# Attention and MLP on one core: block sums moved next to the value matmuls, one x transposed by DMA instead of TensorE, scores of even units one step on

## The chip, the cores and the metric

The kernel runs on 1 core of one Trainium2 chip. The metric is device microseconds of one execution. Before the change the median of 4 runs is 221.29 us (219.48 to 222.63). One execution was profiled; it took 220.52 us, and the profile's span of it, from the first to the last instruction, is 218.8 us.

## What is computed

```python
# q, k, v: (4, 8, 768, 64); block 32, window 16, 24 blocks
k_sum = k.reshape(B, H, nb, block, D).max(axis=3)
v_sum = v.reshape(B, H, nb, block, D).mean(axis=3)
scores_l = scale * q @ k.T          # kept where |i - j| < 16
scores_s = scale * q @ k_sum.T + log(block)
a = softmax(concat(scores_l masked, scores_s))
attn = a @ concat(v, v_sum)
x = attn.transpose(0, 2, 1, 3).reshape(3072, 512)
h = x @ w_in                        # (512, 2048)
out = (h * sigmoid(1.702 * h)) @ w_out
```

## The kernel before

The 3072 rows are cut into 8 units u of 384 rows, half a batch each: b = u // 2, half = u % 2. Each unit has an input stage and an output stage. In the input stage (`ff_in`, line 676) TensorE multiplies `w_in` by the unit's transposed x: 16 groups nt of 4 matmuls with 384 columns, and ScalarE applies the gelu into `gT`. In the output stage (`ff_out`, line 704) TensorE multiplies `gT` by `w_out` into `po`, 48 matmuls with 512 columns in 12 steps of 4; a step is (ms, part), ms being one of three blocks of 128 rows. After part 3 ScalarE copies `po` into `osb` and SP stores it.

The attention of unit u+1 is done inside the output stage of unit u. Function `beside` (line 896) is called after each step i with a plan of tokens for unit u+1: `plan0` for unit 1, `plan1` for unit 2, `odd` for odd units, `plan` for the other even ones. A token is a letter and a number:

- `s0`..`s3`, `S0`, `S1`: the scores of a pair of heads (`scores`, line 624): 24 small matmuls into `ps_s`, an exp on ScalarE into `a_sb`, a mask on VectorE. `s` in an even unit's plan is its own first half; `S` belongs to the odd unit after it.
- `v0`, `v1`: the values of two pairs (`values`, line 634): 24 small matmuls a pair into `ps_av`, then a reciprocal and a multiply on VectorE into `x2`.
- `x0`, `x1`: the x of two pairs is transposed on TensorE and copied by VectorE into `xTT` (`tx`, line 663).
- `d0`, `d1`: the same by a DMA transpose, issued from SP (`dx`, line 671).
- `t0`..`t3`: transposes of q for unit 2 (`tq1`, line 610).

`xTT[0]` holds pairs 0 and 1 and `xTT[1]` pairs 2 and 3. The first matmuls of every input stage read `xTT[0]` (k0 = 0 in `ff_in`).

The order of the work on each engine and on the SP queue is the order in which the program issues it: every call goes through `_Ordered` (line 17), which keeps program order. SP issues all loads, stores and DMA transposes but those of the weights, in one queue. In unit 1's output stage that queue has, in this order: four loads of k for batch 2 (line 1010), the store of ms 0, four loads of v for batch 2 (line 1013), the stores of ms 1 and ms 2. Behind them come the DMA transposes of k, whose input GpSimd casts in unit 2's input stage (`turn_keys`, line 924); GpSimd then casts v there too.

The block sums of v (`vsum`, line 305) are 24 matmuls with a selecting matrix `E` into `ps_vs`; `block_sums` (line 347) copies them into `vs` with four VectorE instructions; `halo_dmas` and `sum_dmas` spread the rows into the next batch's `vw`. In units 2 and 4 all of this stands after step 9 of the output stage (i == 10, line 1018).

`busy(6)` (line 341) is six matmuls of zeros, 128 columns each, ahead of the first output matmul of unit 0.

PSUM is held in pool `psb` (2 buffers, scores, block sums) and pool `pmm` (4 buffers, everything else).

Of the kernel before, what the change touches and what calls it, by code (L numbers as in the profile page):

```python
# [34 lines left out]
def kernel(  # L35
# [10 lines left out]
    B, H, S, D = q.shape  # L46
# [8 lines left out]
    NJ = S // 128  # L55
# [10 lines left out]
    pool = _Ordered(tc, nc.gpsimd)  # L66
# [16 lines left out]
    def chunks(x, b, p):  # L83

        return x[b, 2 * p:2 * p + 2].rearrange("h s d -> (h s) d").rearrange("(a p) d -> p a d", p=128)
# [12 lines left out]
    def load_q(b, p, half=None):  # L98
        if half is None:
            t = stage.tile([128, 2, NJ, D], F32, name=f"qf{p}", tag=f"qf{p}0")  # L100
            sp.dma_start(out=t.rearrange("p h j d -> p (h j) d"), in_=chunks(q, b, p))
            raw["q", p] = t
            return
        if half and p == 0:
            late[0] = stage.tile([128, NP, 2, JH, D], F32, name="qfl", tag="qfl")
            if b == 0:
                pool.dma_start(out=late[0].rearrange("p i h r d -> p (i h) (r d)"),
                               in_=q[0, :, HALF:S].rearrange("h (p r) d -> p h (r d)", r=JH))
        t = (late[0][:, p] if half else
             stage.tile([128, 2, JH, D], F32, name=f"qf{p}0", tag=f"qf{p}0"))  # L110
        raw["q", p, half] = t
        if b == 0 and half:
            return
        sp.dma_start(out=t.rearrange("p h r d -> p h (r d)"),
                     in_=q[b, 2 * p:2 * p + 2, half * HALF:(half + 1) * HALF]
                     .rearrange("h (p r) d -> p h (r d)", r=JH))
# [135 lines left out]
    def copy(eng, out, in_):  # L252
        if eng is act:
            act.activation(out=out, in_=in_, func=ACT.Copy)
        elif eng == "dve_alone":

            dve.tensor_reduce(out=out, in_=in_.unsqueeze(len(in_.shape)), axis=AX.X, op=ALU.max)
        else:
            eng.tensor_copy(out=out, in_=in_)
# [20 lines left out]
    def cast_q(eng, p, half=None):  # L280
        if half is None:
            if p % 2 == 0:
                qb2[p // 2] = castp2.tile([128, 2, NJ, 2, D], BF16, name="qb", tag="qb")
            t = qb2[p // 2][:, p % 2]
        else:
            t = castp.tile([128, JH, 2, D], BF16, name="qb", tag="qb")
        copy(eng, t.rearrange("p r h d -> p h r d"),
             raw[("q", p) if half is None else ("q", p, half)])
        cast["q", p] = t

    def rows_of(s, p, hh=None):

        hs = slice(2 * p, 2 * p + 2) if hh is None else slice(2 * p + hh, 2 * p + hh + 1)
        return vw[s].rearrange("p (j e) h c -> p j e h c", e=2)[:, :, :, hs, 0:D]

    def raw_v(p, hh=None):
        t = raw["v", p] if hh is None else raw["v", p][:, hh:hh + 1]
        return t.rearrange("p h j d -> p j h d")
# [6 lines left out]
    def vsum(s, js):  # L305

        if js[0] == 0:
            vs_ps[0] = psb.tile([128, 1024], F32, name="ps_vs", tag="big")[:, 0:2 * D]
        w5 = vw[s].rearrange("p (j e) h c -> p j e h c", e=2)
        for j in js:  # L310
            o = 20 - 4 * j
            for g in range(4):
                pe.matmul(out=vs_ps[0][32 * g:32 * g + 32, :], lhsT=E[:, o:o + 32],
                          rhs=w5[:, j, 0, 2 * g:2 * g + 2, 0:D],
                          start=(j == 0), stop=(j == NJ - 1), skip_group_check=True)
# [25 lines left out]
    def busy(n):  # L341
        ps = pmm.tile([128, 512], F32, name="ps_w", tag="mm")
        for i in range(n):
            pe.matmul(out=ps[:, 0:128], lhsT=warm[:, 0:128], rhs=warm[:, 0:128],
                      start=True, stop=True)

    def block_sums():
        for g in range(4):
            dve.tensor_copy(out=vs[0:32, 2 * g:2 * g + 2, 0:D],
                            in_=vs_ps[0][32 * g:32 * g + 32, :]  # L350
                            .rearrange("p (h d) -> p h d", d=D))
# [11 lines left out]
    def halo_odd(w5, j0, eng=sp):  # L363
        eng.dma_start(out=w5[32:48, j0:NJ, 1], in_=w5[48:64, j0:NJ, 0])
        eng.dma_start(out=w5[48:64, j0:NJ - 1, 1], in_=w5[0:16, j0 + 1:NJ, 0])
# [131 lines left out]
    def b_exp(g):  # L497
        ab = st["ab", g] = attp.tile([128, HALF], BF16, name="ab", tag="ab")
        act.activation(out=ab, in_=st["B", g][:, 0:HALF], func=ACT.Exp, scale=scale)

    def v_own(p, hh, eng):

        copy(eng, rows_of(0, p, hh)[:, :, 1], raw_v(p, hh))
# [118 lines left out]
    a_sb, x_sb, x2 = {}, {}, {}  # L622
# [107 lines left out]
    gate2 = consts.tile([128, 1], BF16, name="gate2")  # L730
# [149 lines left out]
    for p in range(NP):  # L880
# [2 lines left out]

    plan = {0: ["s0", "s1"], 3: ["v0", "s2", "s3"], 4: ["d0"], 5: ["v1", "S0", "S1", "d1"]}
    odd = {0: ["v0", "s2", "s3"], 1: ["d0"], 3: ["v1", "d1"]}

    plan1 = {0: ["t0"], 1: ["t1"], 2: ["s0", "s1"], 4: ["t2"], 5: ["t3"],
             6: ["v0", "s2", "s3"], 8: ["x0"], 9: ["v1", "S0", "S1"], 11: ["x1"]}  # L890

    plan0 = {-1: ["q0", "q1", "q2", "q3", "s0", "s1"], 3: ["v0", "s2"], 5: ["x0", "s3"], 7: ["v1"], 9: ["x1"]}

# [50 lines left out]
    for u in range(2 * B):  # L944
        b, half = u // 2, u % 2
        todo = {}
        if u == 0:
            for p in range(NP):
                todo.setdefault(12 + p // 2, []).append(lambda p=p: cast_q(dve, p, 1))
        elif u == 1:  # L950
            s = 1
            todo = {2: [lambda: tk(0, s)], 4: [lambda: tk(1, s)],
                    6: [lambda: tk(2, s)], 8: [lambda: tk(3, s)],
                    14: [lambda: halo_odd(w51, 0), lambda: vsum(s, range(NJ))],
                    15: [lambda: block_sums(), lambda: halo_even(w51, 0),
                         lambda: sum_dmas(w51, 0)]}
            for p in range(NP):
                cast_k(pool, p)
            for p in range(NP):
                cast_v(pool, s, p, 0)  # L960
                cast_v(pool, s, p, 1)
            for p in range(NP):
                cast_q1(p)
        elif half == 0 and b + 1 < B:
            todo = {0: [lambda: turn_keys(u, b + 1)]}
        elif b + 1 < B:
            s = (b + 1) % 2
            todo = {0: [lambda: turn_queries(u, s)],
                    1: [lambda: rest_k(0, s)], 3: [lambda: rest_k(1, s)],
                    6: [lambda: rest_k(2, s)], 8: [lambda: rest_k(3, s)]}  # L970
        if u == 1:
            for p in range(NP):
                clear_kx(pool, p, 0)
            clear_vw(pool, 0)
        if u:
            ff_in(u, range(3))
        for nt in range(0 if u else N0, NT):
            if u == 0 or nt > 2:
                ff_in(u, (nt,))
            for f in todo.get(nt, ()):  # L980
                f()
        nxt = u + 1 < 2 * B
        if nxt:
            exp_soon()
        if u == 0:
            beside(1, -1)
            busy(6)
        i = 0
        order = [(ms, part) for ms in range(JH) for part in range(4)]
        if u == 0:  # L990

            order = [(ms, part) for part in range(4) for ms in range(JH)]
        for ms, part in order:
            if nxt or ms < JH - 1:
                ff_out(u, ms, part)
            elif part == 0:
                ff_last(u, ms)
            if nxt:
                beside(u + 1, i)
            i += 1  # L1000
            if u == 0 and i == 1:

                sp.dma_start(out=hold, in_=w_out_sb[0:16, NT - 5, 0:16])
                for p in range(NP):
                    load_k(1, p)
                load_v(1)
                for p in range(NP):
                    load_q(1, p, 0)
                    load_q(1, p, 1)
            elif half and b + 2 < B and i == 1:  # L1010
                for p in range(NP):
                    load_k(b + 2, p)
            elif half and b + 2 < B and i == 7:
                load_v(b + 2)
            elif half == 0 and 0 < b < B - 1 and i == 7:
                for p in range(2, NP):
                    load_q(b + 1, p)
            elif half == 0 and 0 < b < B - 1 and i == 10:
                s = (b + 1) % 2
                vsum(s, range(NJ))  # L1020
                block_sums()
                w5 = vw[s].rearrange("p (j e) h c -> p j e h c", e=2)
                halo_dmas(w5, 0)
                sum_dmas(w5, 0)
# [30 lines left out]
```

The softmax here doesn't subtract the row's maximum and nothing guards it: scores larger than these inputs give would overflow.

## Time and profile before

| what | value |
|---|---|
| median of 4 runs | 221.29 us |
| the profiled execution | 220.52 us |
| its span | 218.8 us |
| PE busy | 205.2 us (94%) |
| ScalarE / VectorE / GpSimd busy | 135.2 / 92.1 / 68.3 us |
| `po` matmuls (377 recorded) | 85.6 us |
| `ph` matmuls (512) | 86.1 us |
| DMA moved | 37.15 MB, mean 170 GB/s |

PE is TensorE's matmuls, PEld its weight loads, DVE VectorE, ACT ScalarE, POOL GpSimd. In a timeline row the columns are start, duration (both us), engine, line, operation, output<-input, shapes and a count; an idle time of the engine before the row and what ended it stand in brackets. SPq is the SP queue; its durations are those of the issuing instruction, and a DMA lands later. Nearly every call has line 27, that of the helper that records the order, so groups are told apart by the names of their tiles. `ps_w` is the work of `busy`, `ps_x` that of `tx`, `ps_vs` that of `vsum`, `ps_s` scores, `ps_av` values. In tile names buffer numbers are left out, so `xT` is either half of x.

### The profile page before, as it was taken

What the parts mean: (1) busy time and instruction counts of PE and PEld (TensorE: products, weight loads), DVE (VectorE), ACT (ScalarE), POOL (GpSimd) and SP (SyncE); (2) the same over time, 40 slices, a digit from 0 to 9 for tenths busy, and PEclk for the clock granted to TensorE, in tenths of its full rate; (3) what the DMA queues carried; (4) which work ended last, traced back from release to release, by engine and by line L of the source; (5) the groups of instructions that cost most, each with busy time, mean ns of one, the idle gap of its engine ahead of it and who ended that gap; (6) DMA issues with size and microseconds to landing.
All of it is one profiled execution on the core that took longest, in us unless ns stands there. A gap on an engine that the chain in (4) does not pass through costs nothing.

```text
span 218.8 us, 4915 instructions
## 1 busy us (share of the span) xinstructions
PE 205.2 (94%) x1927; PEld 116.8 (53%) x1950; DVE 92.1 (42%) x262; ACT 135.2 (62%) x242; POOL 68.3 (31%) x169
## 2 busy tenths in 40 slices
PE   7684999999999999999999999999999999999994
PEld 3353756455655556545555455545655565456542
DVE  5797656553964750335707300619328003300000
ACT  2795778346678487842886677915787578437420
POOL 5683898014794019500600069104100000000000
PEclk9999799999999999999999999999999999999999
DMA  6999799999998999899799999999904300520012
GB/s 171 309 214 196 107 267 204 214 201 221 222 316 229 228 252 240 143 210 236 157 214 220 204 224 196 204 203 208 195 3 101 118 0 3 120 89 10 0 48 96
DMA packets 92710, 37.15 MB, mean 170 GB/s; under 512 B 77856, under 2 KB 89568, under 8 KB 92688
## 3 DMA queue, kind: packets, MB, share of 16 engines
q1 hardware_dynamic: 88272, 31.87, 70.6%
q0 software_dynamic: 4416, 4.98, 13.0%
q8 instruction: 15, 0.25, 0.5%
q14 instruction: 7, 0.06, 0.1%
HBM read 27.26 MB, written 6.29 MB: 153 GB/s over the span
## 4 chain that ended last, share of the span: by engine, by line
PE 86%; DMA 5%; SPq 4%; issue 1%; DVE 1%; POOL 0%; DVEq 0%
PE ph L27 38%; PE po L27 37%; PE ps_av L27 4%; SPq L27 4%; DMA vf<-in_v_dram 3%; PE ps_s L27 3%; DMA kf<-in_k_dram 2%; DVE qT L27 1%; PE ps_x L27 1%; PE ps_q L27 1%; PE ps_vs L27 1%; PE ps_t L27 1%; PE ps_vt L27 0%; POOL vw L27 0%; PE ps_w L27 0%
## 5 line engine op out<-in xcount | busy, mean ns | idle before, releaser
L27 PE MATMUL po<-w_out_sb,gT 128*128 128x512 bf16 (+2 forms) x377 | 85.6, 370 | 2.4 <-issue 1.7
L27 PE MATMUL ph<-xT,w_in_sb 128*128 128x384 bf16 x512 | 86.1, 327 | 0.0
L27 ACT ACTIVATE gT<-ph 128x384 bf16<-128x384 f32 x128 | 61.0, 490 | 22.3 <-PE ph L27 22.2
L27 PEld LDWEIGHTS <-w_in_sb 128*128 128x128 bf16 x512 | 49.8, 98 | 33.1 <-issue 0.4
L27 PEld LDWEIGHTS <-gT 128*128 128x128 bf16 x400 | 36.7, 98 | 38.6
L27 ACT ACTIVATE osb<-po 128x512 f32<-128x512 f32 (+1 forms) x24 | 14.1, 588 | 35.0 <-PE po L27 33.7
L27 ACT ACTIVATE a_sb<-ps_s 128x768 bf16<-128x768 f32 x32 | 24.3, 804 | 11.8 <-PE ps_s L27 11.5
L27 DVE RECIPROCAL rc<-ps_av 128x6 f32<-128x6 f32 x32 | 6.1, 190 | 51.8 <-PE ps_av L27 51.8
L27 POOL CAST vw<-vf 128x768 bf16<-128x768 f32 (+4 forms) x35 | 24.5, 758 | 6.5 <-DMA vf<-in_v_dram 4.9
L27 DVE TENSOR_TENSOR a_sb<-a_sb,mk 128x768 bf16<-128x768 bf16 x32 | 17.9, 559 | 17.5 <-ACT a_sb L27 15.9
L27 ACT ACT_TABLE_LOAD x16 | 20.5, 1283 | 1.1 <-PEq L1039 0.8
L27 POOL COPY gate<-gT 128x1 bf16<-128x1 bf16 x4 | 0.8, 190 | 60.3 <-ACT gT L27 60.3
L27 DVE TENSOR_TENSOR x<-ps_av,rc 128x384 bf16<-128x384 f32 x28 | 15.6, 558 | 1.0
L27 POOL CAST kb<-kf 128x768 bf16<-128x768 f32 (+1 forms) x15 | 11.1, 766 | 15.6 <-DMA kf<-in_k_dram 15.6
L27 DVE COPY osb<-po 128x128 f32<-128x128 f32 x1 | 0.3, 291 | 26.6 <-PE po L27 26.6
L27 PEld LDWEIGHTS <-a_sb 128*64 128x64 bf16 x384 | 8.1, 112 | 6.3 <-issue 3.0
L27 DVE TENSOR_REDUCE ks<-kx 128x24 bf16<-128x768 bf16 x12 | 11.3, 938 | 0.1
L27 DVE COPY kx<-kx 128x80 bf16<-128x80 bf16 (+4 forms) x50 | 11.0, 291 | 0.0
L27 PE MATMUL ps_av<-vw,a_sb 128*64 128x65 bf16 x384 | 10.1, 199 | 0.0
L27 PE MATMUL ps_s<-qT,kx 64*128 64x64 bf16 x384 | 9.3, 191 | 0.8 <-DVE qT L27 0.4
L27 POOL CAST qb<-qf 128x768 bf16<-128x768 f32 (+1 forms) x14 | 9.4, 696 | 0.6 <-POOL qb L27 0.3
L27 PEld LDWEIGHTS <-kx 64*128 64x128 bf16 x384 | 7.0, 95 | 3.5 <-issue 2.7
(71 smaller groups left out, 120.7 us busy)
## 6 DMA issues: line engine op xcount, KB each, us to landing
out_dram<-osb SPq DMA_DIRECT2D x23, 256.0 KB, 3.3
kf<-in_k_dram SPq DMA_DIRECT2D x12, 384.0 KB, 5.5
vf<-in_v_dram SPq DMA_DIRECT2D x12, 384.0 KB, 6.3
qf<-in_q_dram SPq DMA_DIRECT2D x8, 384.0 KB, 4.9
w_in_sb<-in_moe_w_in_dram POOLq DMA_DIRECT2D x4, 512.0 KB, 7.5
w_out_sb<-in_moe_w_out_dram POOLq DMA_DIRECT2D x4, 512.0 KB, 15.4
kf<-in_k_dram SPq DMA_DIRECT2D x8, 192.0 KB, 4.4
qf<-in_q_dram SPq DMA_DIRECT2D x8, 192.0 KB, 3.6
```

The lines of the kernel that those rows point to most:

```text
L27: r = f(*a, **kw)
```

## The change

Five edits and one function that nothing calls:

1. `plan`: `s0`, `s1` stand after step 1 instead of step 0 (units 4 and 6, so in the output stages of units 3 and 5).
2. `plan1`: the first x of unit 2 is transposed by DMA (`d0` after step 7) instead of on TensorE (`x0` after step 8).
3. `busy(6)` is gone.
4. The loads of v for batch 2, in unit 1's output stage, are issued after step 7 instead of after step 6, so behind the store of ms 1 and behind `d0`. (For batch 3 they stay.)
5. In the output stages of units 2 and 4, `vsum` stands after step 3 (right behind `v1`) and `block_sums` after step 4, instead of both after step 9. The DMAs that spread the rows stay after step 9.

```diff
+    def pool_waits(p):
+        pool.tensor_copy(out=gate2, in_=a_sb[p][:, 0, 0, 0:1])
...
-    plan = {0: ["s0", "s1"], 3: ["v0", "s2", "s3"], 4: ["d0"], 5: ["v1", "S0", "S1", "d1"]}
+    plan = {1: ["s0", "s1"], 3: ["v0", "s2", "s3"], 4: ["d0"], 5: ["v1", "S0", "S1", "d1"]}
     odd = {0: ["v0", "s2", "s3"], 1: ["d0"], 3: ["v1", "d1"]}
     plan1 = {0: ["t0"], 1: ["t1"], 2: ["s0", "s1"], 4: ["t2"], 5: ["t3"],
-             6: ["v0", "s2", "s3"], 8: ["x0"], 9: ["v1", "S0", "S1"], 11: ["x1"]}
+             6: ["v0", "s2", "s3"], 7: ["d0"], 9: ["v1", "S0", "S1"], 11: ["x1"]}
...
         if u == 0:
             beside(1, -1)
-            busy(6)
...
-            elif half and b + 2 < B and i == 7:
+            elif half and b + 2 < B and i == (8 if u == 1 else 7):
                 load_v(b + 2)
             elif half == 0 and 0 < b < B - 1 and i == 7:
                 for p in range(2, NP):
                     load_q(b + 1, p)
+            elif half == 0 and 0 < b < B - 1 and i == 4:
+                vsum((b + 1) % 2, range(NJ))
+            elif half == 0 and 0 < b < B - 1 and i == 5:
+                block_sums()
             elif half == 0 and 0 < b < B - 1 and i == 10:
                 s = (b + 1) % 2
-                vsum(s, range(NJ))
-                block_sums()
                 w5 = vw[s].rearrange("p (j e) h c -> p j e h c", e=2)
                 halo_dmas(w5, 0)
                 sum_dmas(w5, 0)
```

In the changed program PE has 24 instructions fewer (12 matmuls and their weight loads), VectorE one fewer (the copy of `ps_x` into `xT`), SP one more (the DMA transpose). ScalarE and GpSimd have the same instructions in the same order.

## The prediction

> **What bounds the kernel now.** I read the page's busy table and slices first, then the chain that ended last, then the timelines of PE and of the SP queue around the edits.
>
> ```profile
> PE 205.2 (94%) x1927; PEld 116.8 (53%) x1950; DVE 92.1 (42%) x262; ACT 135.2 (62%) x242; POOL 68.3 (31%) x169
> ...
> PE   7684999999999999999999999999999999999994
> ...
> PEclk9999799999999999999999999999999999999999
> DMA  6999799999998999899799999999904300520012
> ```
>
> From about 25 us PE is full at full clock, and the DMA engines are full too until about 150 us. So removed PE work is worth its own length, but a PE instruction that comes to depend on a DMA meets a crowded queue. The chain at the end of unit 1's output stage shows it is PE alone:
>
> ```profile
> 76.13 0.50 PE ps_av L27 x24
> 76.63 0.46 PE ps_s L27 x24
> 77.09 0.16 issue
> 77.25 1.67 PE po L27 x7
> 78.92 0.34 PE ps_x L27 x6
> 79.25 10.56 PE ph L27 x64
> ```
>
> Unit 2's input stage (`ph`) starts the moment unit 1's output stage ends. Its first matmuls read the x that the change hands to a DMA. The SP queue there:
>
> ```profile
> 69.29 4.58 SPq L27 DMA_DIRECT2D kf<-in_k_dram  x3
> 73.97 1.68 SPq L27 DMA_DIRECT2D out_dram<-osb  x1
> 75.70 6.88 SPq L27 DMA_DIRECT2D vf<-in_v_dram  x4
> 83.09 1.65 SPq L27 DMA_DIRECT2D out_dram<-osb  x2
> 84.84 6.03 SPq L27 DMA_TRANSPOSE kx<-kb  x4
> ```
>
> SP issues without a pause. The load at 70.54 took 1.56 us to issue and 6.1 us to land; stores behind loads (83.09 and 84.38) landed 4.0 and 3.3 us after issue.
>
> **The change, part by part.**
>
> *busy(6) gone.* The zeros start at 37.85 and the first `po` at 38.19 (PE timeline): 0.34 us of PE removed. Its cover: `po` reads the first quarter of w_out, which lands at 37.2 (issued 25.26, 11.9 to landing), in time. The second quarter lands at 40.5 (26.00 + 14.5); it is first read 12 matmuls of 0.216 us later, at 40.8 before and 40.4 after, so some 0.1 us may go back. No other idle time opens there, so the clock is not touched.
>
> *x0 by DMA.* Six transposes, 78.76 to 79.09 for the like of them (`x1`), 0.33 us, leave PE, and a 0.56 us copy leaves VectorE, off the path. PE would now reach unit 2's first `ph` at 79.09 - 0.34 - 0.33 = 78.4.
>
> When is the x there? Its multiply ends on VectorE at 73.45 + 0.56 = 74.0 (0.3 earlier after). SP is not free: the four k loads and the store of ms 0 hold it until 75.65, and that clock is set by the DMAs, not by PE. Next comes the store of ms 1, which used to stand behind the v loads (its copy ends at 74.9); a second store in a row issues in 0.4 us (84.38). So `d0` starts to issue at about 76.2. Its landing:
>
> ```profile
> L27 SPq DMA_TRANSPOSE xT<-x x10: 1212/1249/3633, 92.7 to 189.2; - x10
> DMA to landing us min/median/max: 2.8/4.2/5.7
> ```
>
> Two of the ten have a recorded landing: 2.8 us with an empty queue (189.24) and 5.7 us behind two loads of q (92.69). They are the ends: 79.0 and 81.9. Between them I follow the queue: the store ahead is issued at 75.7 and lands 3.3 to 4.0 us later, 79.0 to 79.7; a transpose of this size then needs what the k transposes need in a full queue, four in 6.03 us or 1.5 each: 80.5 to 81.2. DMA share backs the far end: 1.28 in 76 to 80 us against 0.81 ahead of the 5.7 us row and 0.26 around the 2.8 us one. I take 80.9, and 0.1 for PE to resume: 81.0. PE stands from 78.4 to 81.0, 2.6 us, and the stage starts 81.0 - 79.09 = **+1.9 us** later. The 0.67 us saved is inside this, as is any loss at 40.4: PE only waits less. Ends: 0.0 (79.0 + 0.1) and +2.9.
>
> The Trainium skill, "VectorE: DVE Perf Modes", section "The three transpose paths", gives 1309 ns for a 128x128 DMA transpose against 390 ns on TensorE, and its rules prefer TensorE where a PSUM destination will do, which speaks against this edit. By its 1.3 us, as an estimate, `d0` would land at 77.5, no wait would arise and the sum would be about 220.2 us on the profiled run. The trace's own shortest is 2.8 us, so the row decides.
>
> *v loads behind d0.* They issue some 0.4 + 1.5 = 1.9 us later. The last lands at 79.81 + 6.6 = 86.4, then 88.3. GpSimd casts k from 81.5 and v from 84.56, eight in 6.25 us; the last pair's casts start at about 89.2, and GpSimd shifts with PE (its gate waits for `gT`), so to 91. Covered by 2 to 3 us; uncovered, it would delay only casts whose first PE reader is the block sums, below. The k transposes behind (84.84) move to about 86.7; VectorE first reads them at 101.7. The `d0` of unit 3 (92.69) is behind them too, but moves with PE. I price all this at nothing.
>
> *Block sums earlier.* They need all v casts: 84.56 + 6.25 = 90.8 against 94.8 at the new place; in unit 4, 137.4 against 141.3. Both 4 us of slack, shifted alike. A PSUM buffer is free (exps end at 93.25). The four copies (1.18 us) move on VectorE from 100.6 to about 96.2, where it idles 4.4 us; `vs` is read by the same DMAs at the same place. PE's price by start-to-start:
>
> ```profile
> 94.26 0.57 PE L27 MATMUL ps_av<-vw,a_sb 128*64 128x65 bf16 x24
> 94.76 1.47 PE L27 MATMUL po<-w_out_sb,gT 128*128 128x512 bf16 x6
> ```
>
> Values alone take 0.50, block sums alone 0.46 (100.04 to 100.50), scores alone 0.46; values with scores behind them take 1.19 (116.74 to 117.93), with a 0.16 us "issue" gap at the end. Joined: 1.19 - 0.96, less 0.09 for the one entry saved (0.31 from the last `po` to a small group against 0.22), so +0.14. Nearest row: 24 values and 24 others without a `po` between. Twice: **+0.3**. Without the gap the join saves up to 0.15 each: -0.3. So -0.3 to +0.3.
>
> *Even scores one step on.* Same PE work. Scores start 0.87 us later, at 114.46; the exp waited for the table load and gate until 114.74 and now starts 0.40 after the scores (as 117.24 to 117.64), at 114.86: 0.12 late. The second mask ended at 116.83, now 116.95, when values (116.74 on) reach the second pair. `v1` at 119.53 shows such a touch: 0.05 us. Twice: **+0.1**, 0 to 0.2.
>
> Sum: 220.5 + 1.9 + 0.3 + 0.1 = 222.8 on the profiled run. That run is 0.8 below the median of the four, so I predict **223.6** against 221.29, +1.0%.
>
> **The rivals.**
>
> *d0 lands in time* (the other side, not slower). For it: the 2.8 us row and x ready at 73.7. If `d0` lands by about 79 us, the start of unit 2 is at -0.6 to 0, with the rest -0.3 to +0.4: 219.6 to 220.9 on the profiled run, about 221.0 by the median. It decides at a landing of 79.0. Against: in-order queue, DMA share 1.28.
>
> *The wait also drops the clock.* This one is worse:
>
> ```profile
> 18.33:21.74 3.41, 0.59 (x15) 0.41 (x13) 2.13 (x7) 1.22 (x3) 1.10 (x3) 1.00 1.23 203
> 21.75:25.16 3.41, 3.32 (x33) 2.57 (x33) 1.41 (x4) 1.79 (x6) 2.74 (x5) 0.50 0.42 55
> ```
>
> PE was idle for 2.92 us (18.92 to 21.84, waiting for a v cast) and then had 3.41 us at clock 0.50 (the last column but two). An idle of 1.34 us at 5.5 left it at 1.00. A 2.6 us wait lies between; half a clock for 3.41 us costs 1.7: 225.3. It decides where a wait fills most of one 3.41 us window; 2.6 us falls wholly in one in a quarter of the phases.
>
> The Trainium skill, "TensorE: Matmul & The Clock Gate", section "Why this matters for your kernels", asks for no gaps over about 3 us. By it 2.6 us costs nothing more, 223.6; the 2.92 us row shows the drop a little below that mark.
>
> *The edit gains over 1%*: would need 2.2 us off PE; the edits remove 0.67. Only noise gives that.
>
> **How the numbers follow.** A late `d0` with the clock kept 0.62, with the clock dropped 0.14, `d0` in time 0.19, else 0.05. The late case's own range, landing 80 to 81.9, is 222.7 to 224.8. About 1% (2.2 us) is what a measurement of this kernel can tell from no change, so its bound is 223.5; the late case lies above it with some 0.44 of its 0.62. Slower: 0.44 + 0.14 = 0.58; same: 0.18 + 0.18 = 0.36; faster: 0.06. Range: 221.1 to 225.4, from the upper half of the case in time to the dropped clock at the middle landing; it leaves out about 0.09 of the case in time, 0.05 of the unnamed and 0.05 of the dropped clock with a late landing.
>
> **What would show it.** A PE gap of 1.5 to 3 us ahead of the first `ph` of unit 2, its wait put down to the DMA into `xT`; SP with two stores, then a DMA_TRANSPOSE at about 76; `ps_vs` straight behind `ps_av` with an "issue" gap; no other new gap. Wrong if `ph` starts by 79 us there, or if any other stage moves by over 0.3 us.

## The result, and the profile after

| | before | after |
|---|---|---|
| median, same chip, turn by turn | 220.25 us (16 runs) | 223.07 us (11 runs) |
| lowest to highest | 217.42 to 222.66 | 220.83 to 226.26 |
| the profiled execution | 220.52 us | 223.65 us |
| its span | 218.8 us | 221.9 us |

The ratio is 1.0151, 95% interval 1.0101 to 1.0202: the kernel became slower by about 1.5%. It is taken over the executions within 1.5% of the fastest of their kernel, so it isn't the quotient of the medians in the table, which are of all executions and give 1.0128. The page of the changed kernel, its busy line and slices:

```profile
PE 206.1 (93%) x1915; PEld 116.1 (52%) x1938; DVE 85.8 (39%) x261; ACT 135.6 (61%) x242; POOL 69.1 (31%) x169
...
PE   7786998999999949999999999999999999999994
...
PEclk9999999999999979999999999999999999999999
```

PE has 12 matmuls fewer than before and yet is busy for 0.9 us longer. Two places differ: slice 15 (77.7 to 83.2 us) has PE at 4 and the clock at 7, and the early clock drop of the kernel before (21.75 to 25.16 us) is absent. The wait list of PE from 30 us on (columns: us in total, times, longest) names the first:

```profile
PE ph L27 <- DMA xT<-x: 3.1, 1, 3.1
PE po L27 <- issue: 2.1, 13, 0.2
PE ps_s L27 <- DVE qT L27: 0.9, 3, 0.4
PE po L27 <- DMA w_out_sb<-in_moe_w_out_dram: 0.5, 2, 0.3
```

The first and the last are new. The `issue` row is no wait: it stands for `po` matmuls whose records are missing (see "Block sums joined" below). The chain of work that ended last passes through the new transpose, and not through PE, at the end of unit 1's output stage:

```profile
75.21 0.46 PE ps_s L27 x24
75.67 0.16 issue
75.82 0.08 PE po L27
75.90 5.02 DMA xT<-x
80.92 0.05 issue
80.97 12.09 PE ph L27 x64
```

The SP queue there:

```profile
68.34 5.19 SPq L27 DMA_DIRECT2D kf<-in_k_dram  x4
73.63 2.16 SPq L27 DMA_DIRECT2D out_dram<-osb  x2
75.90 2.49 SPq L27 DMA_TRANSPOSE xT<-x  x1
78.44 5.66 SPq L27 DMA_DIRECT2D vf<-in_v_dram  x4
84.22 1.68 SPq L27 DMA_DIRECT2D out_dram<-osb  x1
```

Four loads of k, two stores, then the transpose: issued at 75.90, landed at 80.92. PE had finished its other work at 77.83 and stood for 3.14 us. From the first `ph` of unit 2 to the first `po` behind it then took 11.92 us for what took 10.56 before (the chain's 12.09 runs to the end of the last `ph`). Two stretches of 3.41 us show why (us, then PE, PEld, DVE, ACT and POOL busy with counts, granted clock, DMA share, GB/s):

```profile
77.26:80.67 3.41, 0.57 (x8) 0.32 (x5) 0.93 (x2) 1.77 (x3) 0.00 (x0) 1.00 1.16 223
80.68:84.09 3.41, 3.12 (x10) 1.49 (x11) 0.00 (x0) 0.34 (x1) 0.00 (x0) 0.50 1.35 222
```

While PE stood, the clock was 1.00; for the 3.41 us after that it was 0.50, and PE ran 10 matmuls where the next 3.40 us ran 22.

Stage by stage, from the first matmul of a stage to that of the next, in the two profiled executions:

| stage | before | after | difference |
|---|---|---|---|
| start of unit 1's output stage | 63.40 | 62.16 | -1.24 |
| unit 1 output | 15.69 | 18.81 | +3.12 |
| unit 2 input | 10.56 | 11.92 | +1.36 |
| unit 2, unit 4 output | 12.58 each | 12.48 each | -0.10 each |
| unit 3, unit 5 output | 13.12 each | 13.19 each | +0.07 each |

These come to 3.2 of the 3.1 us that the span grew. The -1.24 is no gain of the edits. The first `ph` of unit 0 came 2.53 us earlier (at 22.01 instead of 24.54), because PE waited for 1.43 us instead of 2.92 in the start-up and the clock stayed up, before any instruction that the change touches; `after_again`, the changed kernel once more, has a wait of 3.1 us there and the drop. The two stages of unit 0 then took 1.29 us longer.

### The profile page after: what moved, and what is told of

The parts are those of the page before. It is cut to its first block, busy times and chain, and to the rows that moved or that the text cites. A ratio compares the mean times of both kernels' runs of the same rounds, so it can differ in the third digit from the quotient of the medians.

```text
span 221.9 us, 4892 instructions
## 1 busy us (share of the span) xinstructions
PE 206.1 (93%) x1915; PEld 116.1 (52%) x1938; DVE 85.8 (39%) x261; ACT 135.6 (61%) x242; POOL 69.1 (31%) x169
## 3 DMA queue, kind: packets, MB, share of 16 engines
q1 hardware_dynamic: 89072, 32.06, 72.6%
## 4 chain that ended last, share of the span: by engine, by line
PE 77%; DMA 14%; SPq 3%; POOL 2%; issue 2%; DVE 1%; POOLq 0%; DVEq 0%
PE po L27 35%; PE ph L27 34%; DMA w_out_sb<-in_moe_w_out_dram 7%; SPq L27 3%; PE ps_av L27 3%; PE ps_s L27 3%; DMA vf<-in_v_dram 3%; DMA xT<-x 2%; DMA kf<-in_k_dram 2%; POOL vw L27 1%; PE ps_q L27 1%; DVE qT L27 1%; POOL w_in_sb L27 1%; PE ps_vs L27 1%; PE ps_t L27 1%
## 5 line engine op out<-in xcount | busy, mean ns | idle before, releaser
L27 PE MATMUL ph<-xT,w_in_sb 128*128 128x384 bf16 x512 | 87.2, 330 | 3.3 <-DMA xT<-x 3.1
L27 POOL CAST vw<-vf 128x768 bf16<-128x768 f32 (+4 forms) x35 | 25.1, 776 | 4.2 <-DMA vf<-in_v_dram 3.1
L27 DVE COPY kx<-kx 128x80 bf16<-128x80 bf16 (+4 forms) x50 | 7.8, 249 | 0.0
```

What stands on the lines that cost most here:

```text
L27: r = f(*a, **kw)
```

## The experiments

The theory after the result: the transpose `d0` lands late because of what SP issues ahead of it, and that wait, with a clock drop in some executions, is all of the loss. Rivals: that the other three edits cost a part; that the clock drop, not the wait, is most of it; that not the place in the queue but the transpose by DMA itself is too slow.

All ratios are to the kernel before, run beside it on the same chip, with 95% intervals.

### Which edit

`x_on_pe`: the changed kernel with edits 2 and 4 taken back.

```diff
-             6: ["v0", "s2", "s3"], 7: ["d0"], 9: ["v1", "S0", "S1"], 11: ["x1"]}
+             6: ["v0", "s2", "s3"], 8: ["x0"], 9: ["v1", "S0", "S1"], 11: ["x1"]}
...
-            elif half and b + 2 < B and i == (8 if u == 1 else 7):
+            elif half and b + 2 < B and i == 7:
```

> The changed kernel with the x of unit 2 back on TensorE and the v loads back in their place; the removed busy, the earlier block sums and the later scores stay. Theory 1 (the late DMA transpose is the loss): no PE gap over 0.5 us after 25 us, clock 1.00 from there on, the time within 0.5% of the kernel before, or a little under it (busy -0.3, less a wait for w_out; block sums -0.1 each; scores +0.07 each): about -0.2 us. Theory 2 (the other edits cost as much): still over 1% slower, with the loss in the output stages of units 2 to 5.

Measured: 219.04 us, ratio 0.9999 (0.9966 to 1.0032). Without edits 2 and 4 the loss is gone, and the other three together are worth nothing that can be measured. Its profile has unit 1's output stage at 15.91 us and unit 2's input stage at 10.56.

`d0_only`: the kernel before with edits 2 and 4 alone, the reverse of the diff above.

> The kernel before with only the DMA transpose of unit 2's x and the v loads behind it; busy, block sums and scores as before. Theory 1: the whole loss, +2.5 to +4 us (1.2 to 1.8%), a PE gap of 2 to 3.2 us ahead of the first ph of unit 2, put down to the DMA into xT; half clock after it in a part of the executions. Theory 2: under 1%.

Measured: 222.14 us, ratio 1.0097 (1.0046 to 1.0147). The same wait is there:

```profile
PE ph L27 <- DMA xT<-x: 3.1, 1, 3.1
```

Unit 1's output stage took 18.59 us. Here the clock stayed at 1.00 behind a wait of 3.07 us, and unit 2's input stage took 10.41. So the wait alone makes a loss; the drop need not be there. The times say the same: the six executions of `d0_only` whose mean clock stayed at 1.00 have a median of 220.95 us, and the 20 of the kernel before on that chip with a mean clock of at least 0.996 one of 218.73, 2.2 us less. Edit 4 without edit 2 was not run.

`busy_vsum`: the kernel before with edits 3 and 5 alone (`busy(6)` gone, block sums behind `v1`).

> The kernel before without busy(6) and with the earlier block sums; x on TensorE, scores and v loads as before. The join theory of the prediction (24 values and 24 others side by side cost 0.14 more): units 2 and 4's output stages 12.7 us instead of 12.6. Rival, from the traces since: 0.1 us less each, 12.5. busy: 0.34 us less TensorE work, but a wait for the second quarter of w_out of up to 0.3 in its place. Time: the kernel before within 0.3%.

Measured: 219.24 us, ratio 0.9991 (0.9952 to 1.0030). No effect that can be told from none; what each of the two edits does shows in the stages, below.

### How much is the clock

`fill_wait`, and once more as `fill_again` beside the changed kernel as `after_again`: matmuls of zeros in the wait, which leave the output as it is.

```diff
+        if u == 2:
+            busy(40)
         if u:
             ff_in(u, range(3))
```

> The changed kernel with 40 matmuls of zeros (128 columns, 2.2 us) ahead of unit 2's input stage, so that PE works while it waits for the transpose. Theory 1 with the clock (the idle window halves the clock): the clock stays 1.00 there, unit 2's ph takes 10.5 us instead of 12.1, the stage starts at the same time, and the kernel is faster than the changed one by 0.8 to 1.7 us, so 0.5 to 1.0% slower than before. Rival (the clock drop has another cause, or filler only adds work): ph still 12.1 us or the stage starts over 1 us later; as slow as the changed kernel or slower.

Measured: 222.42 us, ratio 1.0143 (1.0083 to 1.0202).

> The changed kernel with the 40 matmuls of zeros ahead of unit 2's input stage, on the chip of the run beside it. Theory 1 with the clock: no execution with a mean clock under 0.99, and 0.5 to 1.5 us less than the changed kernel in the median. Rival (the drop costs nothing because the DMAs pace unit 2 anyway, or filler costs what it saves): the same median within 0.4 us.

> The changed kernel once more, beside the next run, to set the share of its executions whose clock drops against that with filler. Both theories: 1.0 to 2.0% over the kernel before; mean clock under 0.99 (two drops or more) in about a third of the runs.

Measured: `fill_again` 222.04 us, 1.0118 (1.0060 to 1.0176), and `after_again` 222.89 us, 1.0128 (1.0052 to 1.0204). In `fill_again` the same two stretches are:

```profile
77.40:80.80 3.40, 2.61 (x45) 2.37 (x43) 0.56 (x1) 1.34 (x3) 0.00 (x0) 1.00 1.26 200
80.80:84.20 3.40, 3.40 (x23) 2.04 (x22) 0.00 (x0) 1.92 (x5) 1.50 (x3) 1.00 1.36 221
```

The zeros kept PE busy for 2.61 of the 3.40 us, 0.79 us of wait was left, and the clock stayed at 1.00; unit 2's input stage took 10.41 us in both profiles with the zeros, and 11.92 and 12.09 in the two of the changed kernel. The mean clock of each execution says the same: it was under 0.99 (two drops of 3.41 us or more) in 7 of 18 executions of the changed kernel, in 1 of 12 with the zeros and in 5 of the 69 of the kernel before that ran beside the experiments. That one, at 0.977, I had not expected. The medians of `fill_again` and `after_again` differ by 0.85 us, within the 0.5 to 1.5 that I expected, but each ratio lies within the other's interval, so this is not shown. The runs do resolve that the loss stays when PE is kept busy and the drop behind `d0` is rare: the interval of `fill_again` begins at 1.0060.

### The place in the queue

`half_k_behind`: two of the four loads of k for batch 2 move from ahead of `d0` to behind it.

```diff
-                for p in range(NP):
+                for p in range(2 if u == 1 else NP):
                     load_k(b + 2, p)
...
             elif half and b + 2 < B and i == (8 if u == 1 else 7):
+                for p in range(2, NP if u == 1 else 2):
+                    load_k(b + 2, p)
                 load_v(b + 2)
```

> The changed kernel with two of batch 2's four k loads issued behind the transpose instead of ahead of it, which takes 768 KB (about 3.6 us of transfers) out of the queue ahead. Theory 1 (the transpose is late because of the loads ahead of it in the in-order queue): it lands 3 to 4 us earlier, at about 77 us, the PE gap is under 0.4 us, and the time is that of the kernel before within 0.5%. Rival (the transpose itself takes 4 to 5 us wherever it stands, or the pushed loads make unit 2 wait): the gap stays over 2 us, or a new one over 1 us stands at the block sums of unit 2.

Measured: 219.55 us, ratio 1.0029 (0.9995 to 1.0064). Most of the loss is gone. But the landing was not where I expected it:

```profile
72.66 2.31 PE po L27 x11
74.97 4.57 DMA xT<-x
79.54 0.05 issue
```

`d0` was issued only 0.9 us earlier, since it still stood behind the store of ms 1, whose data came at 74.46, and it landed at 79.54. PE had a gap of 1.10 us, where I had expected less than 0.4.

`d0_first`: as `half_k_behind`, and `d0` is issued ahead of the store of ms 1; edit 1 is taken back.

```diff
-    plan = {1: ["s0", "s1"], 3: ["v0", "s2", "s3"], 4: ["d0"], 5: ["v1", "S0", "S1", "d1"]}
+    plan = {0: ["s0", "s1"], 3: ["v0", "s2", "s3"], 4: ["d0"], 5: ["v1", "S0", "S1", "d1"]}
...
-             6: ["v0", "s2", "s3"], 7: ["d0"], 9: ["v1", "S0", "S1"], 11: ["x1"]}
+             6: ["v0", "d0", "s2", "s3"], 9: ["v1", "S0", "S1"], 11: ["x1"]}
```

> As the changed kernel with two k loads behind the transpose, with the transpose also ahead of the store of ms 1 and right behind the first values (and the scores of even units in their old place). Theory 1 (queue): it issues at about 73.5 us and lands by 77, no PE gap over 0.3 us ahead of unit 2, time 0.1 to 0.5% under the kernel with two k loads behind. Rival (a transpose beside loads takes 4.5 us or more, whatever is ahead): it lands at about 78, gap 0 to 0.8 us.

Measured: 219.55 us, ratio 0.9980 (0.9936 to 1.0023). The SP queue:

```profile
70.84 1.75 SPq L27 DMA_DIRECT2D out_dram<-osb  x1
74.39 1.34 SPq L27 DMA_TRANSPOSE xT<-x  x1
75.85 0.49 SPq L27 DMA_DIRECT2D out_dram<-osb  x1
```

SP was free at 72.6, waited for the x until 74.39, and the transpose landed at 77.28, 2.9 us later; `ph` starts at 79.08 with no wait. A wait appeared elsewhere:

```profile
PE ps_s L27 <- DMA qT<-qb: 0.9, 1, 0.9
```

These are the first scores in unit 3's output stage, at 113.62 to 114.53: q had been issued at 109.43 and landed after 5.05 us. Edit 1 puts these scores one step later, so:

`d0_first_s1`: `d0_first` with edit 1 back in.

> As the kernel with the transpose first, with the scores of even units one step on as in the change. Theory 1: no PE gap ahead of unit 2; the 0.91 us gap that the kernel with the transpose first showed at the scores of unit 4 (113.6 us) is not there, since the scores come 0.87 us later; unit 3's output stage 13.2 us; time the kernel before within 0.5%, at best 0.4% under it. Rival: the gap moves to the scores' new place.

Measured: 218.67 us, ratio 0.9977 (0.9939 to 1.0015). The wait for q is gone; unit 1's output stage took 15.60 us (15.36 in `d0_first`, 18.81 in the changed kernel). This is the lowest ratio of all, and its interval still holds 1, so none of these kernels is shown to beat the kernel before.

`d0_behind_v`: the kernel before with edit 2 alone, so that the four loads of v stay ahead of `d0`.

> The kernel before with the DMA transpose of unit 2's x, but with the v loads in their old place, so four more loads (1.5 MB) ahead of the transpose. Theory 1 (in-order queue): the transpose issues at about 82 us instead of 76 and lands at about 87; PE gap 8 to 9 us; with the clock halved behind it, +9 to +11 us, 4 to 5% slower. Rival (the landing does not depend on the loads ahead): as the change, +2 to 4 us.

Measured: 230.66 us, ratio 1.0521 (1.0461 to 1.0581).

```profile
75.06 6.54 SPq L27 DMA_DIRECT2D vf<-in_v_dram  x4
82.11 0.99 SPq L27 DMA_DIRECT2D out_dram<-osb  x1
83.23 1.38 SPq L27 DMA_TRANSPOSE xT<-x  x1
```

`d0` was issued at 83.23 and landed at 86.78; PE stood for 9.4 us. The clock was at 0.50 for 10.24 us, from 82.10 to 92.34, so for the first 5.5 us behind the wait, and unit 2's input stage took 13.11 us. So edit 4 is what keeps edit 2 from costing 5%.

The same transpose in four places of one queue: landed at 77.28, 79.54, 80.92 and 86.78, ratio 0.998, 1.003, 1.015 and 1.052. The loss follows the landing, so the transpose by DMA is not too slow in itself. (The four kernels differ in edits 1, 3 and 5 too, which `x_on_pe` showed to be worth nothing together.)

## Why the prediction was right, and where it was wrong

**`d0` late: right.** Predicted: issued at 76.2, landed at 80.9. Measured: 75.90 and 80.92. Following the queue (stores first, then a transpose) gave the landing, but that it came out to 0.02 us is luck. The store ahead was to land at 79.0 to 79.7; 15 of its 16 completions came at 79.92 to 80.05. The transpose was then to take 1.5 us; it landed 0.87 us behind the store, and 0.86 to 0.90 us in the four other profiles with this queue. One error was late by about 0.7 us, the other short by about 0.6. The 1.3 us that the Trainium skill states in "VectorE: DVE Perf Modes", section "The three transpose paths", for one 128x128 block (`d0` turns six) is shorter than any landing that these runs recorded (2.8 to 2.9 us at the least, 5.02 here).

**PE's arrival: 0.6 us off, in a way that costs nothing.** I had PE at 78.4; it came at 77.8, the start-up having been quicker. The wait became 3.14 instead of 2.6 us, and the landing stayed. That the landing is set by DMAs and not by PE, as the prediction has it, is argued and not shown: in the five profiles with four loads of k ahead of `d0` it comes 38.3 to 39.3 us after the landing of the third quarter of w_out, but PE's arrival keeps step with that load too (35.7 to 35.8 us behind it in the changed kernel, `after_again` and `d0_only`). If it is so, the 0.67 us taken off PE only lengthen the wait.

**The clock drop: right mechanism, chance too low.** I gave it 0.14 of the 0.76 in which `d0` is late and took the case with the clock kept as the likeliest. The profiled execution had the drop, and it was not rare: the 30 executions of the changed kernel and `d0_only` lost 0.79% of the clock on average, the 69 of the kernel before 0.42%, and one drop is 0.77% of a run (half of 3.41 us in 222). That makes it some 0.5 of the executions, an estimate from few. The step that failed is "2.6 us falls wholly in one in a quarter of the phases": the wait was longer, and it need not be wholly in a window. In the changed kernel 0.57 us of PE work were in the 3.41 us ahead of the drop, in `after_again` 1.25. There a wait of 2.66 us brought a drop, in `d0_only` one of 3.07 us none, so the length alone does not decide, and the mark of about 3 us that the prediction quotes does not sort the two. The Trainium skill, "TensorE: Matmul & The Clock Gate", section "What's actually happening", has a window of 3413 ns that runs freely and does not reset when a kernel starts; both the 3.41 us at 0.50 and the drop's start at 80.68, 0.29 us ahead of PE's return, agree with that, and so do the two drops of `after_again`, at 21.68 and 83.12: they are 61.44 us apart, 18 times 3.413.

**Block sums joined: wrong sign.** I took +0.14 a unit from values with scores behind them. The step that failed is their price of 1.19 us, and with it the 0.16 us "issue" gap: there is no such gap. The profile before has records of 1927 matmuls beside 1950 weight loads, the changed kernel's 1915 beside 1938; in `d0_only` and five other profiles every matmul has its record (1944 beside 1944 in `d0_only`), and no `po` there waits for "issue". One kernel shows both: `fill_wait` with every record and no such gap, `fill_again` with 23 records missing and 13 gaps. The place that the prediction read, in unit 3's output stage, before:

```profile
116.74 0.57 PE L27 MATMUL ps_av<-vw,a_sb 128*64 128x65 bf16 x24
117.24 0.52 PE L27 MATMUL ps_s<-qT,kx 64*128 64x64 bf16 x24
117.93 1.67 PE L27 MATMUL po<-w_out_sb,gT 128*128 128x512 bf16 x7 [0.16 <-issue]
```

The same place in `d0_only`:

```profile
117.78 0.57 PE L27 MATMUL ps_av<-vw,a_sb 128*64 128x65 bf16 x24
118.28 0.52 PE L27 MATMUL ps_s<-qT,kx 64*128 64x64 bf16 x24
118.73 1.90 PE L27 MATMUL po<-w_out_sb,gT 128*128 128x512 bf16 x8
```

(`ps_av x24` is one `v`, 12 matmuls a pair; `ps_s x24` is two `s` of 12 each.) Eight `po` follow, not seven, and they start 0.95 us after the values: the 1.19 held one `po` of 0.22 us without a record. With 0.95 the prediction's own sum gives 0.95 - 0.96 - 0.09 = -0.10, and that is what was measured: the output stages of units 2 and 4 went from 12.58 to 12.48 us, in every profile with edit 5 and in none without. The -0.09 is the one change from 512-column to small matmuls that the join saves.

**Even scores: right.** +0.05 each predicted, +0.07 measured, 0.3 of a per mille each, and in the place foreseen: the first values of unit 3's output stage took 0.57 us to the scores behind them, 0.50 before.

**`busy(6)`: the size was off.** I took -0.34, of which perhaps 0.1 would come back. In the profiled execution all of it came back, and more: PE waits for w_out, 0.18 us for the first quarter and 0.32 for the second.

```profile
24.38 15.13 DMA w_out_sb<-in_moe_w_out_dram
39.51 0.04 issue
39.55 1.02 PE po L27 x4
```

Unit 0's output stage took 12.91, 12.91 and 13.13 us in the three profiles with `busy(6)` in it (before, `d0_only` and `d0_behind_v`). It took 13.40 and 13.50 in the two of the changed kernel, but 13.00 and 13.08 in `x_on_pe` and `busy_vsum`, where about 0.1 came back as predicted. So the load that I named as the next bound can take the gain, and does not always. None of this can be told from nothing in the time, as `busy_vsum` shows.

**v behind `d0`, priced at nothing: held.** No wait for a v cast stands in the wait list of the changed kernel.

Predicted were 223.6 us and +1.0%, measured 223.07 and a ratio of 1.0151. The sum on the profiled run was 222.8 and it took 223.65: +1.36 for the dropped clock that the sum did not have, -0.5 for the two block sums and +0.04 for the even scores make 223.7. That the time lies near the prediction is in part luck, then, since an error of +1.4 and one of -0.5 stand against each other. Of the signs of being wrong one came true, a stage that moves by over 0.3 us: unit 2's input stage moved by 1.36, which the rival with the dropped clock had foreseen, and unit 0's two stages by 0.80 and 0.49.

**How much is wait and how much clock.** By the executions without a drop the wait is about 2 of the 2.8 us between the medians: 2.2 us in `d0_only`, above, and 2.0 in `after_again` (a median of 221.43 us over 3 executions with a mean clock of at least 0.996, against 219.46 over 10 of the kernel before on that chip). The rest goes with the clock, and these few executions do not give its size.

**What stays open.** Why `half_k_behind`'s transpose took 4.57 us when that of `d0_first`, issued 0.6 us earlier, took 2.9; see the last section.

## What to carry to other kernels

A transfer that replaces work on the bounding engine is worth what it lands at, and that is read from its queue: list what the same queue issues ahead of it, take the landing of a neighbour in the same crowd, and compare it with the moment the engine arrives. If it lands later, removing more work from that engine can only lengthen its wait, and the cure is in the queue: here two loads and one store put behind the transpose took 3.6 us off its landing and brought the time back. Before you count a small gain at the start of a stage, look for the load that lands next; it may become the bound. And before you price a gap that waits for nothing, count the instructions around it: a record may be missing.

## What the runs showed of the hardware that I had not expected

A DMA transpose has 16 completions in these traces, PE waits for the last, and one can be far behind. In `half_k_behind` 15 of them came at 77.80 to 77.92 and the last at 79.54. A packet of the instruction queue (16 KB) ran there from 77.49, for 0.96 us; in the changed kernel such a packet began at 76.28 and took 1.65 us; in `d0_first` and `d0_first_s1`, where the transpose took 2.9 us, none ran between its issue and its landing. The queue table of the changed kernel from 76 to 79.5 us (packets, MB, share of 16 engines):

```profile
q1 hardware_dynamic: 1626, 0.86, 129.3%
q8 instruction: 1, 0.02, 3.0%
```

And from 79 to 79.7 us the view shows hardly a packet, though the transpose landed only at 80.92:

```profile
DMA  9990030000300030000300030000300000100010
...
q1 hardware_dynamic: 21, 0.02, 29.8%
```

This view counts the packets that begin in its window, so it does not say that the DMA engines were free. By the packet records 20 packets of 256 bytes, which began at 78.60 to 79.04, ended only at 79.86 to 79.90, where the others of that size took some 0.02 us, while a few of 2 KB ran one after another until 79.58.

That the program's own instruction fetch delays the transpose is my reading of these packets. The records do not say which engine a packet ran on, and no run took the fetch away, so it is not shown.
